# Score steps of all pairs in one row, two to a visit, and P V of two pairs at once, in a fused attention and feed-forward kernel

## The chip, the cores and the metric

One core of a Trainium2 chip runs the whole kernel. The metric is device time in microseconds (us) of one execution; the quoted times are medians. The profile is of one execution.

## The reference

Blockwise causal attention over 8 batches, 8 heads, 576 positions, head size 64 (blocks of 64), then RMS norm and a SwiGLU feed-forward network (FFN) of 512 to 1536 to 512 on all 4608 tokens:

```python
scores = scale * np.matmul(q, k.transpose(0, 1, 3, 2))
scores = np.where(block_i >= block_j, scores, -1000000000.0)
...
attn = attn / (np.sum(attn, axis=-1, keepdims=True) + 1e-09)
x = (attn @ v)                       # (B, S, H*D) as (4608, 512)
rms = np.sqrt(np.mean(x * x, axis=-1, keepdims=True) + 1e-06)
xn = x / rms * rms_g
g = xn @ w_gate
return (g * (1.0 / (1.0 + np.exp(-g))) * (xn @ w_val)) @ w_out
```

## The kernel before

TensorE does everything large: the scores (64 rows of the array for one head, both heads of a pair at once), P V (64 columns for one head, both at once), the column sums, and the FFN (the whole array). In PSUM, the memory that TensorE writes to, the kernel holds two score buffers of two banks each (`ps_s`) and four banks for everything else (`ps_f`). The program is written in the order in which each engine runs it. A "visit" is a piece of attention put between FFN groups; a "group" is one FFN up step (8 matmuls of 512 columns) or one down projection (12 of them). A "pair" is two heads, four pairs to a batch. A "score step" is one of three parts of a pair's scores; the "end blocks" are the first and the last diagonal block of all four pairs, and the "head product" is their P V for the first block. The "corner memsets" set to zero what the mask removes.

In the profile's lines `sps` is a score buffer and `fps` one of the four other banks; `PT` is the exponentials, `OT` the result of P V; `th`, `gs` and `HT` are the steps of an FFN up step (tanh, gate, product); `st` is the norm factors to be spread and `XT` the scaled tokens.

```python
STEPS = {
    0: ([(0, 64, 512, 0)], 0, 512),
    1: ([(1, 128, 448, 0)], 512, 448),
    2: ([(2, 256, 320, 0), (3, 384, 192, 320)], 960, 512), ...
}
ps_s = ctx.enter_context(tc.tile_pool(name="ps_s", bufs=2, space=bass.MemoryType.PSUM))
ps_f = ctx.enter_context(tc.tile_pool(name="ps_f", bufs=4, space=bass.MemoryType.PSUM))
...
def values_mm(b, t, part=WHOLE, early=False):
    chunks, j0, width = part
    clear_pair(b, t)                 # corner memsets that are still due
    ...
    if early:
        ov = ps_f.tile([P, 512], FP32, name="fps")
    else:
        ob = ps_s.tile([P, 2, 512], FP32, name="sps")
        ov = ob[:, 0, :]
    ...                              # ten matmuls, 64 columns of the array each
def evacuate(outs, early=False):
    for o, sq, i in outs:
        if early:
            nc.vector.tensor_copy(out=o, in_=i)
        else:
            nc.scalar.copy(out=o, in_=i)
    for o, sq, i in outs:
        nc.vector.tensor_mul(out=sq, in0=o, in1=o)
...
for b, t in pairs:                   # batches 2 to 7, cut to what matters
    e0 = scores_mm(b, t, 0)
    e1 = scores_mm(b, t, 1)
    scores_exp(*e0)
    group()
    scores_exp(*e1)
    if b > 3 or b == 3 and t == 0:
        group()
    e2 = scores_mm(b, t, 2)
    last = (b, t - 1) if t else (b - 1, HP - 1)
    outs = values_mm(*last, early=b == 2) if b > 3 or t else []
    scores_exp(*e2)
    group()
    evacuate(outs, b == 2)
    if t == 0:
        if b > 3:
            later(1, late_tail if b > 4 else tail, b - 1)
        scores_ends(b)
    if b > 3 or t == 0:
        group()
```

`tail` spreads a batch's norm factors with TensorE; `late_tail` sends them through DRAM by DMA. In both the sums go to VectorE, which takes reciprocal and ratio, splits the result in three BF16 terms (from batch 2 on), and after a small matmul takes the root by Newton steps.

The softmax here doesn't subtract the row's maximum and nothing guards it: scores larger than these inputs give would overflow.

## Time and profile before

| | before |
|---|---|
| time | 399.22 us median (399.04 to 399.74, 4 runs) |
| span in the profile | 397.7 us |
| TensorE, VectorE, ScalarE busy | 96%, 64%, 50% |
| granted TensorE clock | 1.0 |

A line of the timeline begins with its start and its duration, and a bracket at its end gives the idle time of the engine just before it and what ended it. And in a line of the waits "0.9, 2, 0.6" is the total in us, the number of waits and the longest.

### The profile page before, as it was taken

How to read it: one execution, taken by the hardware profiler on the slowest of the kernel's cores; microseconds unless marked ns; L12 is line 12 of the kernel's file. 1: busy time of each engine (PE TensorE's matmuls, PEld its weight loads, DVE VectorE, ACT ScalarE, POOL GpSimd, SP SyncE). 2: the span in 40 equal slices, each digit the busy share in tenths (PEclk: the TensorE clock that was granted, in tenths of full speed). 3: DMA queues.
4: the chain of work that ended last, by engine and by line, in shares of the span. 5: the costliest groups of instructions: out<-in, count | busy, mean ns of one | idle time of the engine just before them, and what ended most of it. 6: DMA issues, size and time to landing. Idle time of an engine off the chain costs nothing.

```text
span 397.7 us, 7820 instructions
## 1 busy us (share of the span) xinstructions
PE 381.0 (96%) x3064; PEld 180.8 (45%) x3064; DVE 254.8 (64%) x640; ACT 197.3 (50%) x285; POOL 128.3 (32%) x181
## 2 busy tenths in 40 slices
PE   8889899999989999999999999999999899999996
PEld 3457665444434444344444444444344344444443
DVE  4788676567967578657716786478638967654430
ACT  3825871466548655455546564566453233332321
POOL 8927764846039204207446700100020010100000
PEclk9999999999999999999999999999999999999999
DMA  8999999999949919609999995200230020100112
GB/s 110 167 202 190 193 145 153 160 152 163 149 49 135 151 29 92 82 0 120 187 148 153 136 117 114 81 2 1 78 104 2 15 86 28 26 29 26 50 38 98
DMA packets 142677, 39.38 MB, mean 99 GB/s; under 512 B 129457, under 2 KB 139953, under 8 KB 142641
## 3 DMA queue, kind: packets, MB, share of 16 engines
q0 software_dynamic: 108448, 26.75, 69.3%
q1 hardware_dynamic: 33504, 12.00, 19.3%
q8 instruction: 24, 0.39, 0.4%
q10 hardware_dynamic: 688, 0.13, 0.2%
q14 instruction: 13, 0.10, 0.1%
HBM read 41.16 MB, written 10.03 MB: 129 GB/s over the span
## 4 chain that ended last, share of the span: by engine, by line
PE 76%; DVE 11%; DMA 5%; POOL 3%; ACT 2%; issue 1%; DVEq 0%; POOLq 0%
PE fps L496 39%; PE fps L521 23%; PE sps L244 5%; PE sps L293 4%; DMA WG<-in_moe_w_gate_dram 3%; DVE HT L504 3%; DVE gs L502 2%; PE fps L333 2%; DMA nt<-in_q_dram 2%; PE fps L293 1%; POOL VB L126 1%; POOL nt L112 1%; DVE st L426 1%; ACT PT L253 1%; ACT th L500 1%
## 5 line engine op out<-in xcount | busy, mean ns | idle before, releaser
L496 PE MATMUL fps<-XT,WG 128*128 128x512 bf16 (+1 forms) x480 | 112.1, 359 | 3.9 <-DVE gs L502 1.9
L502 DVE SCALAR_TENSOR_TENSOR gs<-th,fps 128x512 bf16<-128x512 f32 x108 | 73.9, 684 | 58.4 <-ACT th L500 58.2
L496 PE MATMUL fps<-XT,WV 128*128 128x512 bf16 (+1 forms) x480 | 111.0, 358 | 0.0
L253 ACT ACTIVATE PT<-sps 128x1024 bf16<-128x1024 f32 (+1 forms) x96 | 93.2, 988 | 30.7 <-PE sps L244 30.3
L500 ACT ACTIVATE th<-fps 128x512 f32<-128x512 f32 x108 | 64.6, 598 | 77.1 <-PE fps L496 74.1
L521 PE MATMUL fps<-WO,HT 128*128 128x512 bf16 (+1 forms) x444 | 97.1, 373 | 0.1
L504 DVE TENSOR_TENSOR HT<-gs,fps 128x512 bf16<-128x512 bf16 x108 | 74.3, 688 | 12.3 <-PE fps L496 0.9
L496 PEld LDWEIGHTS <-WV 128*128 128x128 bf16 x480 | 46.9, 98 | 47.1 <-issue 1.0
L496 PEld LDWEIGHTS <-WG 128*128 128x128 bf16 x480 | 42.4, 97 | 52.4 <-issue 17.2
L521 PEld LDWEIGHTS <-HT 128*128 128x128 bf16 x444 | 42.6, 98 | 50.5 <-issue 3.0
L525 POOL DMA_DIRECT2D out_dram<-osb x22 | 12.6, 571 | 153.2 <-ACT osb L523 151.3
L523 ACT ACTIVATE osb<-fps 128x512 f32<-128x512 f32 (+1 forms) x37 | 21.7, 586 | 78.7 <-PE fps L521 68.6
L126 POOL DMA_DIRECT2D VB<-in_v_dram x48 | 39.5, 847 | 6.0 <-DMA nt<-in_q_dram 2.7
L244 PE MATMUL sps<-QT,KT 64*128 64x192 bf16 (+5 forms) x280 | 32.3, 308 | 3.1 <-DVE KT L209 1.0
L119 POOL DMA_DIRECT2D nt<-in_q_dram x30 | 26.3, 876 | 7.0 <-DMA VB<-in_v_dram 4.0
L119 POOL DMA_DIRECT2D nt<-in_k_dram x30 | 26.3, 877 | 6.5 <-DMA VB<-in_v_dram 2.9
L319 DVE TENSOR_TENSOR SQ<-OT 128x512 bf16<-128x512 bf16 (+1 forms) x44 | 15.9, 372 | 10.2 <-ACT OT L317 9.3
L293 PEld LDWEIGHTS <-VB 128*64 128x64 bf16 x344 | 14.5, 109 | 13.1 <-issue 5.2
L441 DVE SCALAR_TENSOR_TENSOR XT<-OT,gscale,fps 128x64 bf16<-128x64 bf16 (+5 forms) x36 | 15.0, 477 | 8.0 <-PE fps L448 8.0
L244 PEld LDWEIGHTS <-KT 64*128 64x128 bf16 x280 | 8.8, 94 | 24.8 <-issue 19.6
L529 POOL DMA_DIRECT2D out_dram<-osb x12 | 6.5, 544 | 41.3 <-ACT osb L523 41.3
L226 DVE MEMSET PT<- 64x64 uint32 x95 | 8.9, 112 | 14.3 <-ACT PT L253 11.1
(77 smaller groups left out, 227.7 us busy)
## 6 DMA issues: line engine op xcount, KB each, us to landing
out_dram<-osb POOLq DMA_DIRECT2D x22, 256.0 KB, 2.4
VB<-in_v_dram POOLq DMA_DIRECT2D x32, 128.0 KB, 6.1
nt<-in_q_dram POOLq DMA_DIRECT2D x24, 128.0 KB, 6.7
nt<-in_k_dram POOLq DMA_DIRECT2D x24, 128.0 KB, 7.3
bc<-rows SPq DMA_DIRECT2D x8, 288.0 KB, 4.7
WG<-in_moe_w_gate_dram POOLq DMA_DIRECT2D x4, 384.0 KB, 9.6
WV<-in_moe_w_val_dram POOLq DMA_DIRECT2D x4, 384.0 KB, 10.8
WO<-in_moe_w_out_dram POOLq DMA_DIRECT2D x4, 384.0 KB, 7.8
```

What stands on the lines that cost most here:

```text
L119: nc.gpsimd.dma_start(out=nt[0:rows, 0:512].rearrange("p (h d) -> p h d", h=H), in_=src[b, :, c * P:c * P + rows, :].rearrange("h p d -> p ...
L126: nc.gpsimd.dma_start(out=vb[r:r + n, cc, :].rearrange("p (h d) -> p h d", h=H), in_=v[b, :, tok:tok + n, :].rearrange("h p d -> p h d"))
L244: nc.tensor.matmul(sp[:, a, o:o + w], KT[b][r, t, c * P:(c + 1) * P], QT[b][r, t, q0:q0 + w], start=True, stop=True, skip_group_check=True)
L253: nc.scalar.activation(out=pt[:, :, lo:lo + width], in_=sp[:, :, 0:width], func=AF.Exp, scale=SCALE)
L293: nc.tensor.matmul(ov[a * D:(a + 1) * D, o:o + w], vb[:, c, h * D:(h + 1) * D], rhs, start=(i == 0), stop=(i == len(chunks) - 1), skip_gro ...
L319: nc.vector.tensor_mul(out=sq, in0=o, in1=o)
L496: nc.tensor.matmul(acc[:, i * w:(i + 1) * w], wt[c][:, p, r * P:(r + 1) * P], XT[:, p, x0:x0 + w], start=(p == 0), stop=(p == HP - 1), ski ...
L500: nc.scalar.activation(out=th, in_=g, func=AF.Tanh, scale=0.5)
L502: nc.vector.scalar_tensor_tensor(out=gs, in0=th, scalar=1.0, in1=g, op0=ALU.add, op1=ALU.mult)
L504: nc.vector.tensor_mul(out=HT[n][:, m:m + k, lo:lo + w], in0=gs.rearrange("p (k w) -> p k w", k=k), in1=u.rearrange("p (k w) -> p k w", k=k))
L521: nc.tensor.matmul(po[:, 0:step], HT[n][:, m, i * P:(i + 1) * P], WO[:, m, o:o + step], start=(m == 0), stop=(m == NMC - 1))
L523: nc.scalar.mul(out=osb[:, o:o + step], in_=po[:, 0:step], mul=0.5)
```

## The change

The intent is to switch TensorE between attention and FFN less often. From batch 3 on the score steps (and the end blocks) of all pairs stand in one row; each visit takes the next two, whatever pair they belong to. P V waits until two pairs are complete, goes to the FFN's banks, and leaves its two score buffers to the scores. Of its copies one goes to ScalarE, the others to VectorE. Batch 3's factors go by DMA like the later ones, and the tail of batches 1 and 2 starts its Newton steps and spread one group earlier.

```diff
@@ tail
-        later(3, norm_newton, b, 0)
-        later(3, norm_newton, b, 1)
-        later(4, norm_spread, b)
+        later(2, norm_newton, b, 0)
+        later(2, norm_newton, b, 1)
+        later(3, norm_spread, b)
@@ the loop over batches 3 to 7 (batch 2 keeps its loop)
+    steps = []
+    for b in range(3, B):
+        for t in range(HP):
+            steps += [(b, t, u) for u in range(3)] + [(b, 0, None)] * (t == 0)
+    def values_of_two():
+        outs = []
+        for b, t in (complete.pop(0), complete.pop(0)):
+            outs += values_mm(b, t, early=True)
+            if t == 1:
+                outs.append(head_product(b, ps_f.tile([P, 512], FP32, name="fps")))
+            if t == HP - 1:
+                sums.append(b)
+        for i, o in enumerate(outs):
+            evacuate([o], i != 1)
+    for i in range(0, len(steps), 2):
+        two = steps[i:i + 2]
+        if sums:
+            late_tail(sums.pop())
+        es = [scores_mm(*x) if x[2] is not None else scores_ends_mm(x[0]) for x in two]
+        if len(complete) > 1:
+            values_of_two()
+        complete += [x[0:2] for x in two if x[2] == 2]
+        b = two[0][0]
+        want += 10 / 6.5 if b == 3 else 16 / 6.5
+        for n in range(max(1, int(want) - given)):
+            if es:
+                scores_exp(*es.pop(0))
+            group()
+            given += 1
+        for e in es:
+            scores_exp(*e)
+        fetch(b + 1, 2)
... (the old loop's lines removed; scores_ends split in matmuls and exponential; some lines cut)
```

More of the change, by code (lines that the diff above doesn't have):

```diff
@@ L249, in scores_exp @@
     def scores_exp(pair, sp, step):
+        if step is None:
+            nc.scalar.activation(out=P4[pair].rearrange("p a t d -> p a (t d)"),
+                                 in_=sp[:, :, 0:HP * BLK], func=AF.Exp, scale=SCALE)
+            return
         parts, lo, width = STEPS[step]
@@ L259, in scores_ends, with scores_ends_mm @@
     def scores_ends(b):
+        scores_exp(*scores_ends_mm(b))
+    def scores_ends_mm(b):
         P4[b] = p4pool.tile([P, 2, HP, BLK], BF16, name="P4")
@@ L269, in scores_ends @@
                                      start=True, stop=True, skip_group_check=True)
-        nc.scalar.activation(out=P4[b].rearrange("p a t d -> p a (t d)"),
-                             in_=sp[:, :, 0:HP * BLK], func=AF.Exp, scale=SCALE)
+        return b, sp, None
     def values(b, t, part=WHOLE, early=False):
@@ L733 @@
         fetch(3, 2)
-    pairs = [(b, t) for b in range(2, B) for t in range(HP)]
-    for b, t in pairs:
-        if (b, t) == (3, 0):
-            values(2, HP - 1, early=True)
-            evacuate([head_product(2, ps_f.tile([P, 512], FP32, name="fps"))], True)
-            later(1, tail, 2, 4)
-        e0 = scores_mm(b, t, 0)
-        e1 = scores_mm(b, t, 1)
+    for t in range(HP):
+        e0 = scores_mm(2, t, 0)
+        e1 = scores_mm(2, t, 1)
         scores_exp(*e0)
@@ L746 @@
         scores_exp(*e1)
-        if b > 3 or b == 3 and t == 0:
-            group()
-        fetch(b + 1, 2)
-        e2 = scores_mm(b, t, 2)
-        last = (b, t - 1) if t else (b - 1, HP - 1)
-        outs = values_mm(*last, early=b == 2) if b > 3 or t else []
+        fetch(3, 2)
+        e2 = scores_mm(2, t, 2)
+        outs = values_mm(2, t - 1, early=True) if t else []
         scores_exp(*e2)
-        if (b, t) == (2, HP - 1):
+        if t == HP - 1:
             clear()
         group()
-        evacuate(outs, b == 2)
+        evacuate(outs, True)
         if t == 0:
-            if b > 3:
-                later(1, late_tail if b > 4 else tail, b - 1)
-            scores_ends(b)
-        if b > 3 or t == 0:
+            scores_ends(2)
             group()
+        fetch(3, 2)
+    values(2, HP - 1, early=True)
+    evacuate([head_product(2, ps_f.tile([P, 512], FP32, name="fps"))], True)
+    later(1, tail, 2, 4)
+    steps = []
+    for b in range(3, B):
+        for t in range(HP):
+            steps += [(b, t, u) for u in range(3)] + [(b, 0, None)] * (t == 0)
+    complete, sums = [], []
+    want = given = 0
+    def values_of_two():
[4 more added lines that the diff above has]
+                outs.append(head_product(b, ps_f.tile([P, 512], FP32, name="fps")))
+            if t == HP - 1:
+                sums.append(b)
[18 more added lines that the diff above has]
+            scores_exp(*e)
         fetch(b + 1, 2)
     group()
-    values(*pairs[-1])
-    later(1, late_tail, B - 1)
+    values_of_two()
+    group()
+    late_tail(sums.pop())
     while di < len(downs):
```

## The prediction

> **What bounds the kernel now.** I read the page first (busy shares, then the slices), then the waits of TensorE, then its timeline in one steady stretch, then the groups by shape, to price what moves.
>
> ```profile
> PE 381.0 (96%) x3064; PEld 180.8 (45%) x3064; DVE 254.8 (64%) x640; ACT 197.3 (50%) x285; POOL 128.3 (32%) x181
> ```
>
> TensorE is occupied in 96% of the span; no other engine is over 64%. That number alone does not say that TensorE has nothing to lose, because a matmul's record is longer than its share of the array. So I look at starts, not at durations, in the timeline of TensorE alone (columns: start us, us, engine, line, operation, output and inputs, tile, shape, count):
>
> ```profile
> 218.73 1.03 PE L496 MATMUL fps<-XT,WG 128*128 128x512 bf16 x4
> 219.59 1.03 PE L496 MATMUL fps<-XT,WV 128*128 128x512 bf16 x4
> 220.55 0.39 PE L244 MATMUL sps<-QT,KT 64*128 64x320 bf16 x4
> 220.87 0.22 PE L293 MATMUL sps<-P,VB 128*64 128x64 bf16 x2
> 220.93 0.79 PE L293 MATMUL sps<-PT,VB 128*64 128x512 bf16 x8
> 221.55 0.29 PE L306 MATMUL sps<-P,VB 128*64 128x64 bf16 x8
> 221.78 1.04 PE L496 MATMUL fps<-XT,WG 128*128 128x512 bf16 x4
> ```
>
> Four FFN matmuls of 512 columns take 219.59 - 218.73 = 0.86 us from start to start, 0.216 us each. The first block of this excerpt therefore should end at 219.59 + 0.86 = 220.45; the scores start at 220.55, 0.10 us late. The score step (320 and 192 columns, two heads at once on two halves of the rows) is worth 512 columns, 0.22 us, so 220.77; P V starts at 220.87, again 0.10 late. P V of one pair streams 64 + 512 + 448 + 320 + 192 = 1536 columns, 0.65 us, and the head product 256 columns, 0.11 us; with the small step between them (221.55 instead of 221.52) that ends at 221.66, and the FFN resumes at 221.78, 0.12 late. So each change of the tile form (128*128, 64*128, 128*64) costs TensorE about 0.11 us in which nothing streams, and no wait is recorded for it. The other loss is real waiting, which the waits of TensorE between 100 and 322 us (batch 2's end to the last of the attention) show:
>
> ```profile
> PE fps L496 <- DVE gs L502: 1.9, 3, 0.8
> PE fps L448 <- DVE st L426: 1.0, 1, 1.0
> PE fps L496 <- DVE HT L504: 0.9, 2, 0.6
> PE sps L293 <- ACT PT L253: 0.5, 2, 0.3
> PE fps L496 <- DVE XT L441: 0.5, 2, 0.3
> PE sps L244 <- ACT OT L317: 0.4, 1, 0.4
> ```
>
> That is 5.2 us in 11 waits. As a record lasts 0.38 us against a pitch of 0.216, each wait hides up to 0.16 us more, so 7 us is an upper estimate. After 322 us TensorE runs FFN alone without any loss: whatever is gained before is gained at the end too.
>
> **What the Trainium skill says.** "TensorEngine Tiling (Array Packing)", section Key Properties, says that changing the tiling mode, not just the tile, drains the engine; the trace agrees, with 0.10 to 0.12 us a change. "TensorE: Matmul & The Clock Gate", section Wait — 56ns, not 53.3ns?, gives 215.7 ns for back-to-back matmuls of 512 columns with a warm clock; the trace has 216. "Perfetto Trace Analysis", section Identifying the Most-Contended Engine, warns that matmul busy share is no measure of headroom and that weight-load busy share is better: 45% here against 96%, which is why I count starts.
>
> **The change, part by part.** In the order of instructions, which can be read without running it, TensorE issues 3047 matmuls after against 3055 before, and changes the tile form 176 times against 206. By kind: FFN to scores 44 for 52, scores to P V 20 for 30, P V to FFN 19 for 29, FFN to or from the end blocks' scores 6 for 13, those beside scores or sums 8 for 1, and two fewer after the sums. Two score steps to a visit was already the rule for steps 0 and 1; what is new is that step 2 and the end blocks share visits too, and that two pairs' P V share one. 30 changes less x 0.11 = 3.3 us, all on the engine that sets the end.
>
> The eight matmuls that go are the spreading of batch 3's factors (four of 512 and four of 64 columns): 4 x 0.216 + 4 x 0.03 = 1.0 us of TensorE. By DMA the factors take about 5 us to land, but batch 3's tokens are wanted ten groups after the sums, some 20 us, so nothing waits.
>
> What moves between the other engines:
>
> ```profile
> L253 ACT ACTIVATE PT<-sps 128x1024 bf16<-128x1024 f32 x64 | 65.2, 1025 | 28.3 <-PE sps L244 27.9
> L504 DVE TENSOR_TENSOR HT<-gs,fps 128x512 bf16<-128x512 bf16 x108 | 74.3, 688 | 12.3 <-PE fps L496 0.9 <-DVE gs L502 0.5
> L502 DVE SCALAR_TENSOR_TENSOR gs<-th,fps 128x512 bf16<-128x512 f32 x108 | 73.9, 684 | 58.4 <-ACT th L500 58.2
> L317 ACT CAST OT<-sps 128x512 bf16<-128x512 f32 x20 | 11.6, 580 | 1.2 <-PE sps L306 1.2
> L315 DVE CAST OT<-fps 128x512 bf16<-128x512 f32 x8 | 5.5, 688 | 0.1
> ```
>
> Of 20 copies of P V on ScalarE ten stay; ten (0.69 us each) and the five head copies (0.42 each, by the 256-column form of the same copy) go to VectorE: +9 us on VectorE, less about 1 us because batch 3's scaling runs as four passes of 0.81 instead of eight pieces of 0.74 and 0.28. VectorE comes to some 263 us, 66%: no bound overall, but it is the engine for which TensorE waits most.
>
> Now the waits. (1) Batch 2's tail: its root, Newton steps and spread are issued one group earlier, and a down projection (2.6 us without VectorE work) now stands before the first spreading matmul. The 1.0 us wait on st should go. (2) P V leaves the two score buffers, so the waits of 0.4 and 0.5 us on ScalarE in batch 3 go. In their place: where a visit has only one FFN group, its second exponential is issued after that group, and ScalarE needs 1.02 + 0.60 + 1.02 = 2.6 us for exponential, tanh, exponential, while TensorE is back at the second score buffer after 1.73 + 0.6 + 0.2 = 2.5 us, with about 0.4 us of start-up on top. Three such visits in batch 3: 3 x 0.4 = 1.2 us. (3) The norm chains. After the sums VectorE does 3.0 us (transpose, reciprocal, three-way split), later 2.9 us more. For batches 4 and 6 the new order then has eight up groups with no down projection between: VectorE needs 8 x 1.39 + 5.9 + about 0.8 for corner memsets = 17.8 us, TensorE 8 x 1.73 + about 2 of scores = 15.8; with about 1.1 us of slack in the four banks I expect some 1.0 us of wait for each. Batches 3 and 5 have a down projection after three groups: 0.2 each. Batch 7 has one just before its sums and one after three groups, where the old order had eight up groups in a row: 0.6 in place of about 2. (4) P V directly after one up group reads corners whose memset queues behind that group's two VectorE passes: 0.3 us, at three places. (5) Banks: P V and head product take two or three of the four FFN banks, but by my reckoning of the rotation each is freed 0.2 to 1 us before its turn. Some 1.5 us are left for smaller misses. Sum of waits after: 1.2 + 2.0 + 0.4 + 0.6 + 0.9 + 1.5 = 6.6 against up to 7: about -0.5.
>
> Total: 399.26 - 3.3 - 1.0 - 0.5 = 394.5 us, 1.2% less.
>
> **Rivals.** A: VectorE and the shared banks become the bound. For it: FFN waits on gs and HT are already the largest entry above, and 9 us of copies go exactly to that engine. Against: VectorE is at 64%, and ScalarE sheds 8 us, so tanh comes sooner. If each of the ten P V visits cost 0.5 us and each norm chain 0.5 us more, the gain would be eaten: 394.5 + 5 + 2 = 401. B: the waits mostly vanish with the changes, since the down projections are placed better: 399.26 - 3.3 - 1.0 - 5 = 390. Against it: five norm chains remain, and the number of groups for each visit is about the same. C: the drain is not paid per change but covered by waiting that is there anyway in batch 3: then only half of the 3.3 is gained, 396.5. The clean starts above, in a stretch without waits, speak against it.
>
> **Range and chances.** The switch count and the matmul count are firm (4.3 us); the waits can go either way by 3 us. Range 391.3 to 398.3. Over 2% faster needs less than 391.3, that is nearly all waits gone: 0.11. Slower by over 2% (407) needs waits of 8 us more than now: 0.02. Within 2%: 0.87.
>
> **What would show it.** Right: start-to-start gaps around a P V visit of two pairs are still 0.10 to 0.12 us at each change of form; the wait on st and those on ScalarE's OT and PT are gone; TensorE's waits on gs and HT sum to 3 to 5 us, the largest in the runs of eight up groups of batches 4 and 6; VectorE's busy time is 261 to 265 us; the attention's last matmul comes at a point after which TensorE streams FFN without loss. Wrong: TensorE waiting on VectorE's OT copies (banks), on score buffers in batches 4 to 7, or a wait on the factors' DMA before the FFN of batch 3.

## The result, and the profile after

The changed kernel takes 392.36 us median (392.07 to 394.07, 4 runs) against 399.22 us. The ratio of the fast runs is 0.9835, with a 95% interval of 0.9805 to 0.9865. Such a ratio is the mean time of one kernel's fast runs over that of the other's of the same rounds, so it is not quite the ratio of the medians. The profiled run of the changed kernel is the slowest of the four, 394.07 us: TensorE's granted clock was 0.91 in its first 20 us, before anything changed, against 1.00 in the kernel before. The comparison below therefore starts at batch 3.

The busy shares of the page after:

```profile
PE 374.6 (95%) x3017; PEld 182.4 (46%) x3056; DVE 265.1 (68%) x651; ACT 189.6 (48%) x270; POOL 128.7 (33%) x181
```

VectorE has 10.3 us more, ScalarE 7.7 less. Next, a P V visit of two pairs in TensorE's timeline after, in the same columns as in the prediction:

```profile
192.98 1.03 PE L502 MATMUL fps<-XT,WV 128*128 128x512 bf16 x4
193.94 0.58 PE L244 MATMUL sps<-QT,KT 64*128 64x448 bf16 x6
194.45 0.22 PE L299 MATMUL fps<-P,VB 128*64 128x64 bf16 x2
194.50 0.79 PE L299 MATMUL fps<-PT,VB 128*64 128x512 bf16 x8
195.13 0.20 PE L299 MATMUL fps<-P,VB 128*64 128x64 bf16 x2
195.16 0.79 PE L299 MATMUL fps<-PT,VB 128*64 128x512 bf16 x8
195.79 0.29 PE L312 MATMUL fps<-P,VB 128*64 128x64 bf16 x8
196.01 1.25 PE L527 MATMUL fps<-WO,HT 128*128 128x512 bf16 x4
```

The FFN ends at 192.98 + 0.86 = 193.84 and the scores start 0.10 us later. They are two steps (448, 320 and 192 columns: 960, 0.40 us), so they end at 194.34, and P V starts 0.11 later. Between the first pair's P V (194.45) and the second's (195.13) there are 0.68 us, of which 0.65 are columns: without a change of tile form the join is nearly free. Three changes serve two score steps and two pairs. The waits of TensorE between 100 and 322 us after:

```profile
PE fps L502 <- DVE HT L510: 1.4, 3, 0.6
PE sps L244 <- ACT PT L257: 0.9, 2, 0.5
PE fps L454 <- DVE st L432: 0.3, 1, 0.3
PE fps L502 <- issue: 0.2, 1, 0.2
PE fps L401 <- DVE gs L508: 0.2, 1, 0.2
```

They sum to 3.0 us in 8 waits, where the kernel before had 5.2 in 11. The 0.2 us on "issue" are no wait: the block at 133.34 shows three records where such a block has four, and the next block starts three paces of 0.216 us later, at 133.98, so the first record is missing from the trace. The wait on gs was the largest and is nearly gone; st fell from 1.0 to 0.3, and the waits for P V's copies on ScalarE have vanished.

To see all of the time at once I went through TensorE's records from the first score of batch 3 to the end. The time of a block of matmuls is the start of the next block less its own start. Its columns are worth N / 2.4 ns + 2.5 ns a matmul, which is the rate that the Trainium skill gives for an isolated matmul ("TensorE: Matmul & The Clock Gate", section Back-to-back issue gap) and which the trace confirms with 0.216 us for 512 in a stream; matmuls on different tiles of the array count once, and a record missing from a block of known size is put back. What a change of tile form takes beyond that, up to 0.14 us, is booked as the change; the rest is waiting.

| from batch 3 on, us | before | after | difference |
|---|---|---|---|
| columns | 273.3 | 272.4 | -1.0 |
| changes of tile form | 13.4 (118) | 9.8 (88) | -3.6 |
| waits | 7.8 | 5.5 | -2.3 |
| sum | 294.5 | 287.7 | -6.8 |

The sum agrees with the 6.9 us between the medians (differences are taken before rounding). Where a change of form and a small wait meet, the line between them is a matter of booking; only their sum is measured.

### The profile page after: what moved, and what is told of

It reads as the page before. It is cut to its first block, busy times and chain, and to the rows that moved or that the text cites. A ratio compares the mean times of both kernels' runs of the same rounds, so it can differ in the third digit from the quotient of the medians.

```text
span 392.3 us, 7763 instructions
## 1 busy us (share of the span) xinstructions
PE 374.6 (95%) x3017; PEld 182.4 (46%) x3056; DVE 265.1 (68%) x651; ACT 189.6 (48%) x270; POOL 128.7 (33%) x181
## 4 chain that ended last, share of the span: by engine, by line
PE 81%; DVE 10%; ACT 2%; DMA 2%; issue 2%; POOL 2%; DVEq 0%; POOLq 0%
PE fps L502 43%; PE fps L527 23%; PE fps L299 6%; PE sps L244 5%; DVE HT L510 3%; PE fps L339 2%; DMA VB<-in_v_dram 2%; DVE gs L508 2%; ACT PT L257 1%; POOL nt L112 1%; DVE tr L370 1%; ACT th L506 1%; DVE OT L321 1%; PE fps L454 1%; DVE SQ L325 1%
## 5 line engine op out<-in xcount | busy, mean ns | idle before, releaser
L502 PE MATMUL fps<-XT,WG 128*128 128x512 bf16 (+1 forms) x466 | 110.6, 358 | 3.0 <-DVE HT L510 1.9
L502 PE MATMUL fps<-XT,WV 128*128 128x512 bf16 (+1 forms) x467 | 109.5, 357 | 0.6
L527 PE MATMUL fps<-WO,HT 128*128 128x512 bf16 (+1 forms) x434 | 96.1, 373 | 0.5
L502 PEld LDWEIGHTS <-WG 128*128 128x128 bf16 x480 | 43.4, 98 | 50.0 <-issue 11.3
L244 PE MATMUL sps<-QT,KT 64*128 64x192 bf16 (+5 forms) x280 | 31.5, 311 | 3.3 <-ACT PT L257 1.3
L299 PE MATMUL fps<-PT,VB 128*64 128x192 bf16 (+5 forms) x280 | 25.8, 315 | 1.6 <-DMA VB<-in_v_dram 1.5
L299 PEld LDWEIGHTS <-VB 128*64 128x64 bf16 x344 | 15.2, 112 | 13.4 <-issue 6.1
L321 DVE CAST OT<-fps 128x512 bf16<-128x512 f32 (+1 forms) x34 | 19.0, 562 | 2.0 <-PE fps L299 1.8
L483 DVE SCALAR_TENSOR_TENSOR XT<-OT,gscale,bc 128x576 bf16<-128x576 bf16 (+2 forms) x24 | 15.7, 714 | 2.8 <-DMA bc<-rows 2.7
```

The source lines that it names most:

```text
L244: nc.tensor.matmul(sp[:, a, o:o + w], KT[b][r, t, c * P:(c + 1) * P], QT[b][r, t, q0:q0 + w], start=True, stop=True, skip_group_check=True)
L299: nc.tensor.matmul(ov[a * D:(a + 1) * D, o:o + w], vb[:, c, h * D:(h + 1) * D], rhs, start=(i == 0), stop=(i == len(chunks) - 1), skip_gro ...
L502: nc.tensor.matmul(acc[:, i * w:(i + 1) * w], wt[c][:, p, r * P:(r + 1) * P], XT[:, p, x0:x0 + w], start=(p == 0), stop=(p == HP - 1), ski ...
L527: nc.tensor.matmul(po[:, 0:step], HT[n][:, m, i * P:(i + 1) * P], WO[:, m, o:o + step], start=(m == 0), stop=(m == NMC - 1))
```

## The experiments

In each, everything that is not in the diff is as in the kernel named. All results were correct, and times are medians. The kernel before took 399.4 to 399.6 us in the same rounds. "Waits" and "changes" are those of the table above, from batch 3 on.

**Changes of form added, and a control.** Both edit the changed kernel's end, where TensorE runs the FFN alone.

```diff
     while di < len(downs):
         group()
+        if not due:
+            sp = ps_s.tile([P, 2, 512], FP32, name="sps")
+            for a in range(2):
+                r = slice(a * D, (a + 1) * D)
+                nc.tensor.matmul(sp[:, a, 0:BLK], KT[B - 1][r, 0, 0:P], QT[B - 1][r, 0, 0:BLK], ...)
```

The control has one matmul over all 128 rows instead: `nc.tensor.matmul(sp[:, 0, 0:BLK], KT[B - 1][:, 0, 0:P], QT[B - 1][:, 0, 0:BLK], ...)`.

> The changed kernel with two score-shaped matmuls of 64 columns (64*128, two row halves, result never read) after each of the last 35 FFN groups, where TensorE otherwise runs without loss; tile forms change 69 more times. Theory of 0.11 us a change: 35 x 0.03 us of columns + 69 x 0.11 = +8.6 us, 401 us. Rival that a change is free and only columns count: +1.0 us, 393.4.

> The control of the run with added changes of form: one full-array matmul of 64 columns after each of the same 35 groups, no change of form. Both theories: 35 x 0.03 = +1.0 us, 393.4. If it costs as much as the other, the price is that of a foreign matmul and not of the form.

Measured: 400.61 us with the changes of form, 393.20 us in the control, that is +8.25 and +0.84 us on 392.36. The 69 changes account for the difference, 7.41 us, 0.107 us each. TensorE's timeline with the changes:

```profile
352.07 1.03 PE L502 MATMUL fps<-XT,WV 128*128 128x512 bf16 x4
353.02 0.20 PE L812 MATMUL sps<-QT,KT 64*128 64x64 bf16 x2
353.16 1.04 PE L502 MATMUL fps<-XT,WG 128*128 128x512 bf16 x4
```

and in the control:

```profile
354.52 1.03 PE L502 MATMUL fps<-XT,WV 128*128 128x512 bf16 x4
355.38 0.19 PE L810 MATMUL sps<-QT,KT 128*128 128x64 bf16 x1
355.41 0.81 PE L502 MATMUL fps<-XT,WG 128*128 128x512 bf16 x3
```

From the start of one FFN block to the next there are 1.09 us with two changes and 0.89 without. The price of a change is shown; the foreign matmul itself costs only its columns. That the run with changes has two matmuls where the control has one does not matter: the second of each two starts 3 to 4 ns after the first.

**The score steps in visits by pair again, P V still of two pairs.** On the changed kernel:

```diff
-            steps += [(b, t, u) for u in range(3)] + [(b, 0, None)] * (t == 0)
+            steps += [[(b, t, 0), (b, t, 1)], [(b, t, 2)] + [(b, 0, None)] * (t == 0)]
-    for i in range(0, len(steps), 2):
-        two = steps[i:i + 2]
+    for two in steps:
-        want += 10 / 6.5 if b == 3 else 16 / 6.5
+        want += 10 / 8 if b == 3 else 16 / 8
```

> The changed kernel with eight visits to a batch, steps 0 and 1 in one and step 2 (with the end block for the first pair) in another, as before; P V still of two pairs. Tile forms change 190 times for 176. Theory of 0.11 us a change: 392.3 + 1.5 = 393.8 us, perhaps 0.5 less as batch 3's visits are met by more even groups. Rival that a change costs nothing: 392.3.

Measured: 391.86 us (ratio 0.9809, 0.9796 to 0.9823), no slower than the changed kernel. The changes did cost 1.45 us more (102 for 88), as expected; but the waits fell from 5.5 to 3.6 us. With 16 groups on eight visits every visit of batches 4 to 7 has two, and no wait over 0.1 us is left in batches 4 to 6. What waiting is left there is mostly in batch 2's tail and batch 7's norm chain. So the row of steps, the part of the change that gave it its name, brings nothing on balance: what it saves in changes it gives back in uneven visits.

**P V of one pair to a visit.** On the changed kernel:

```diff
-        for b, t in (complete.pop(0), complete.pop(0)):
-            outs += values_mm(b, t, early=True)
-            ...
-            evacuate([o], i != 1)
+        b, t = complete.pop(0)
+        outs = values_mm(b, t, early=True)
+        ...
+            evacuate([o], i != 0 or t % 2 == 0)
-        if len(complete) > 1:
+        if complete and complete[0][0] in ended:   # end blocks' exponential issued in an earlier visit
```

> The changed kernel with P V of one pair to a visit, still in FFN banks and with the same engines for the copies: tile forms change 186 times for 176. Theory of about 0.11 us a change: 392.3 + 1.1 = 393.4 us. Rival that the gain came from waits removed and a change costs nothing of its own: 392.3 or less, as fewer FFN banks are held at once.

Measured: 397.46 us (0.9939 to 0.9964), 5.1 us more than the changed kernel, where both theories were far off. In the table's booking its ten changes cost 1.5 us and its waits 3.7 us (9.25 for 5.54); at 0.107 us each the changes would be 1.1, and the rest small waits beside them. TensorE's waits between 100 and 322 us:

```profile
PE fps L502 <- DVE OT L321: 0.9, 2, 0.5
PE fps L299 <- DVE PT L226: 0.9, 2, 0.4
PE fps L299 <- DVE PT L231: 0.7, 1, 0.7
```

These three kinds are new: P V waits for the corner memsets of its own pair, which stand in VectorE's queue behind FFN passes, and the FFN waits for banks that P V's copies hold. The obvious theory was that P V stands too close behind its exponential. A last run tested it.

```diff
-        if complete and complete[0][0] in ended:
+        if complete and complete[0][2] < i - 2 and complete[0][0] in ended:   # one visit later
-    ppool = ... bufs=5
+    ppool = ... bufs=6
```

> The run with P V of one pair to a visit (397.5 us, 4 us more than its ten extra changes of form explain), but each pair's P V one visit later, with a sixth buffer for the exponentials; still 186 changes. Theory that those 4 us are P V standing too close behind its own exponential and corner memsets: the waits on PT go, 393.4 to 394.5 us. Rival that single P V visits cost by themselves (their copies and banks): 397 us again.

Measured: 397.86 us (0.9944 to 0.9971). The theory falls. The waits on PT are indeed gone from P V, but as much waiting stands elsewhere (9.6 us in all):

```profile
PE fps L502 <- DVE gs L508: 2.5, 3, 0.9
PE sps L244 <- ACT PT L257: 2.4, 3, 1.7
PE fps L502 <- DVE HT L510: 1.1, 2, 0.6
```

Moving P V also moved the sums and the down projections, so the two runs do not isolate one cause. That P V of single pairs costs some 5 us in this order is shown; why all of it does stays open. No run undid the move of P V from the score buffers to the FFN's banks alone, so what that part is worth stays open too.

**Batch 3's factors by DMA, alone.** On the kernel before: `later(1, late_tail, b - 1)` in place of `later(1, late_tail if b > 4 else tail, b - 1)`.

> Only the kernel before with batch 3's factors by DMA: eight matmuls fewer (1.0 us of columns). Theory that TensorE's stream sets the time: 398.2 us, and up to 0.8 us less where the wait near 160 us was for batch 3's scaling (397.4). Rival that the eight matmuls stood beside other waits: 399.2.

Measured: 397.77 us (0.9945 to 0.9972), -1.7 us against the kernel before in the same rounds (399.46). Columns fell by 1.0 us and waits by 0.65; the wait of 0.8 us of one FFN group for batch 3's scaling is gone.

**The earlier Newton steps, alone.** On the kernel before, only the first hunk of the diff.

> Only the kernel before with batch 2's (and 1's) Newton steps and spread issued one group earlier; tile forms change 206 times as before. Theory that the waits of batch 2's tail are a separate part of the gain: the 1.0 us wait on st goes, 398.2 us (-1.0). Rival that this wait only moves to the next transfer or VectorE pass: within 0.3 us of before, 399.2.

Measured: 399.67 us, ratio 1.000 (0.9988 to 1.0013): no gain, the rival was right. TensorE's timeline at the place:

```profile
113.75 0.39 PE L521 MATMUL fps<-WO,HT 128*128 128x512 bf16 x1 [0.34 <-DVE HT L504]
114.66 0.59 PE L448 MATMUL fps<-st,SELB 128*128 128x512 bf16 x2 [0.53 <-DVE st L426]
```

The spreading waits 0.53 us for st, where it waited 1.0; but the Newton steps now stand in VectorE's queue ahead of gs and HT of the last up step, and the down projection waits 0.34 us for that HT. The first spreading matmul starts at 114.66, before at 114.52.

**All copies of P V on ScalarE.** On the changed kernel: `evacuate([o], False)` for `evacuate([o], i != 1)`.

> The changed kernel with all P V and head copies of batches 3 to 7 on ScalarE. Theory that VectorE's extra 9 us are off the path except in the norm chains: within 0.7 us, 391.6 to 393, with waits moving from VectorE's gs and HT to ScalarE's exponentials. Rival A that VectorE's load is what keeps the gain down: 390 or less.

Measured: 392.82 us (0.9819 to 0.9846), within 0.5 us. VectorE is busy 257.4 us instead of 265.1, ScalarE 196.7 instead of 189.6; the waits are 5.6 for 5.5 us. Rival A of the prediction is out: VectorE's extra copies do not hold the gain down, and no wait for a bank that such a copy holds is among the waits of the changed kernel above.

**Both exponentials before a lone group.** On the changed kernel, where a visit has one group, both exponentials are issued before it.

```diff
+        todo = max(1, int(want) - given)
+        for n in range(todo):
+            while es and (n == 0 or todo > 1):
+                scores_exp(*es.pop(0))
+                if todo > 1:
+                    break
```

> The changed kernel, but where a visit has one FFN group both exponentials are issued before it. Theory that the waits of 0.79 and 0.72 us at score buffers in batch 3 come from the second exponential queueing behind that group's tanh: those two go, 392.3 - 1.3 = 391.0. Rival that ScalarE is simply short of time there: tanh is late instead, FFN waits, 392.3.

Measured: 392.87 us (0.9820 to 0.9850). No gain. TensorE's waits between 100 and 322 us:

```profile
PE fps L502 <- DVE HT L510: 1.4, 3, 0.6
PE fps L454 <- DVE st L432: 0.8, 1, 0.8
PE fps L299 <- DVE PT L226: 0.4, 1, 0.4
PE fps L401 <- DVE gs L508: 0.4, 2, 0.2
```

The waits of scores on ScalarE's PT (0.9) are gone, as foreseen. In their place st waits 0.8 for 0.3, P V waits 0.4 for a corner memset, and gs 0.2 more. I read this as too little FFN around batch 3, with its ten groups, to hide the chains, so that a wait taken away there comes back as another; no run tests that reading.

**FP32 sums, a shorter norm chain.** On the changed kernel: `norm_ratio(b)` for `norm_ratio(b, True)` in `late_tail`.

> The changed kernel, but batches 3 to 7 hand their mean squares to TensorE in FP32 (two terms, GSUM) in place of three BF16 terms: seven short VectorE passes (1.3 us) fewer in each norm chain, some 0.2 us more on TensorE. Theory that the 0.76 + 0.2 us after the root's matmuls in batches 4, 6 and 7 are VectorE's chain holding up gs and HT: those shrink to about 0.2, 392.3 - 2 + 1 = 391.3 us. Rival that they are a fixed price of the small matmul: 393.

Measured: 391.22 us (0.9777 to 0.9807), the fastest kernel; waits and columns together fall by 1.4 us. After the sums of batch 4, TensorE and VectorE in the changed kernel:

```profile
181.32 0.22 PE L401 MATMUL fps<-wt,GSUMB 128*128 128x18 bf16 x3
181.37 0.69 DVE L510 TENSOR_TENSOR HT<-gs,fps 128x512 bf16<-128x512 bf16 x1
182.11 1.02 PE L502 MATMUL fps<-XT,WG 128*128 128x512 bf16 x4 [0.57 <-DVE HT L510]
```

and with FP32 sums:

```profile
179.21 0.69 DVE L510 TENSOR_TENSOR HT<-gs,fps 128x512 bf16<-128x512 bf16 x1
...
180.18 0.52 PE L401 MATMUL fps<-w,GSUM 128*128 128x18 f32 x4
...
180.54 1.02 PE L502 MATMUL fps<-XT,WG 128*128 128x512 bf16 x4
```

In the changed kernel the FFN's bank was held until HT ended at 182.06, as HT had queued behind the three-way split; with FP32 sums HT ends at 179.90, long before the bank's turn. The same edit on the run with visits by pair, which had such a wait only in batch 7:

> The run with eight visits to a batch (391.9 us), with the FP32 sums. It has only batch 7's waits (0.76 + 0.3) left in the chains: VectorE theory 391.4; if the FP32 matmuls cost more than they save where nothing waited, 392.5.

Measured: 392.15 us, 0.3 us more than without it, and the intervals overlap. These two runs also show what the FP32 matmuls cost: from their start to the scores behind them 0.45 us (180.52 to 180.97), where the three BF16 ones took 0.16 (180.58 to 180.74) without FP32 sums. That is 0.29 us a chain, or an estimated 1.5 us for five chains, against about 1.0 us of batch 7's waits that go. On the changed kernel the same 1.5 us bought some 2.7 us of waits. In these two orders the FP32 matmuls pay where a chain holds up the FFN and not elsewhere.

**Batch 2's factors by DMA too.** On the changed kernel: `later(1, late_tail, 2, 6)` for `later(1, tail, 2, 4)`, with `late_tail(b, k=9)` applying after k and k + 1 groups.

> The changed kernel with batch 2's factors by DMA too, applied after six and seven groups. Eight matmuls fewer (1.0 us), and the waits at the spreading (0.5 us beside D, 0.3 on st) go: 391.0 us. Rival: its tokens are needed at once after seven groups, and the FFN waits on the scaling or on the transfer instead: 392.3 or more.

Measured: 395.95 us (0.9895 to 0.9953), 3.6 us more. The rival was right in outcome. With the tokens of batch 2 late there are groups with no FFN work to give, and two visits meet:

```profile
127.43 0.39 PE L244 MATMUL sps<-QT,KT 64*128 64x320 bf16 x4
129.43 0.39 PE L244 MATMUL sps<-QT,KT 64*128 64x512 bf16 x2 [1.60 <-ACT PT L257]
```

Between the two score blocks no FFN stands, and TensorE waits 1.60 us for a score buffer.

## Why the prediction was right or wrong

The time was predicted as 394.5 us in a range of 391.3 to 398.3, within 2%; it came out at 392.36, within both, so the prediction was right. Its terms:

- **Changes of form**: 3.3 us expected from 30 changes, 3.6 found in the records, and 0.107 us each measured by themselves. Right. Rival C, that a change is not paid for, is out.
- **Columns**: 1.0 us expected, 1.0 found; the factors' edit alone gave 1.7 us, as the wait for batch 3's scaling went with it.
- **Waits**: this term was mis-sized: -0.5 us expected, -2.3 found, and that is nearly all of the 2.1 us between 394.5 and 392.36. With the changes of form taken out at 0.107 us each, the waits that it foresaw at the norm chains and the score buffers were nearly right, 4.2 us expected and 4.0 found: the norm chains 1.0 and 1.0 (batches 4 and 6), 0.4 (batches 3 and 5) and 0.6 (batch 7) expected, and 0.9, 0.5, 0.3 and 1.0 found; batch 3's score buffers 1.2 expected, 1.3 found. Wrong was what came on top. Of 0.9 us for P V behind its memsets nothing came: after nine of the ten P V visits the next block starts 0.13 us late, no more than the change of form, and the tenth seems 0.35 us late only because the first record of the block behind it is missing (0.216 us of it). Of the 1.5 us "for smaller misses" 0.3 came. In return 1.2 us around batch 2's tail stayed, for which the sum had nothing. And the waits before were 7.8 us where 7 was taken as the most: 0.8 of them stood at batch 3's scaling, which the list of waits shows as 0.5.
- **Batch 2's tail**: the step "The 1.0 us wait on st should go" named the wrong cause. Its earlier Newton steps alone gave nothing. The records around batch 2's chain show 1.2 us of loss after against 1.9 before, and it may be the down projection now ahead of the spreading that helps; no run isolates that.
- **The signs that it named**: the gaps at the changes of form are 0.10 to 0.11 us, as said, and none of the signs of being wrong came (no wait on OT's banks, on score buffers in batches 4 to 7, or on the factors' DMA). But the wait on st did not go wholly (0.3 left), and the waits on gs and HT are 1.6 us in the list of waits where 3 to 5 were expected, the largest in batches 7 and 4 and not in 4 and 6.
- **Busy time**: VectorE at 261 to 265 us expected, 265.1 found.
- **Slips**: by its own terms rival C is 394.5 + 1.65 = 396.1 us, not 396.5, and rival A 401.5. Its counts of matmuls, 3047 and 3055, are nine below the weight loads on the two pages, 3056 and 3064; the difference of eight holds.

Not foreseen at all: that the row of steps would be worth nothing on balance, and P V of single pairs would be 5 us worse. That the total stayed in the range is partly luck: 2.1 us of waits that were feared and did not come stand against 1.2 that were not foreseen and stayed.

## What to carry to other kernels

Where one engine is nearly always busy, subtract the useful work from start-to-start times and name what is left: here 13 us of changes of form and 8 us of waits from batch 3 on. Group small work by the array's tile form, but check with the parts undone one at a time whether uneven spacing gives the saving back. A wait removed by moving work came back as another wait beside it in three runs here (the Newton steps, P V one visit later, both exponentials first). Shortening the chain that causes it, as with the FP32 sums, lasted on the changed kernel, and bought nothing where the chain held up little.

## What the Trainium skill lacked or had wrong

- "TensorEngine Tiling (Array Packing)", section Key Properties, says that a change of tiling mode drains the engine but gives no price. Here 69 changes cost 7.41 us, 0.107 us each, beside full-array matmuls of 512 columns.
- "TensorE: Matmul & The Clock Gate", section Back-to-back issue gap, gives about 131 ns a matmul of 512 columns as sustained pace of weight-load and matmul pairs. Every such stream in these traces, with a weight load for each matmul, runs at 0.216 us, the page's figure for the isolated gap.
- No page gives a time for a small FP32 matmul among BF16 ones; "FP8 and Floating Point Precision" counts the passes of an FP32 matmul without one. Two of 18 columns, which the trace shows as four records, took 0.45 us from their start to the scores behind them (180.52 to 180.97 in the run by pair with FP32 sums), where three BF16 ones took 0.16 us (180.58 to 180.74 in the run by pair), a change of form in both.
